# Five accumulator banks and three gate banks in the last stage of an attention, soft-MoE and SwiGLU kernel, with four smaller moves

## The chip, the cores and the metric

The kernel runs on one core of one Trainium2 chip. Times are device microseconds (us) of one execution. The core has a matrix engine (TensorE, PE in the listings, with its weight loads as PEld), VectorE (DVE), ScalarE (ACT), GpSimd (POOL) and a queue that issues the DMAs (SP). Each engine runs its own instructions in order and waits for the others by semaphores. Matmul results go to PSUM, which has eight banks of 512 fp32 numbers on each of 128 partitions.

## The reference

Three stages, all on 4608 tokens of width 512:

```python
# 1. attention in chunks of 64 rows, 64 heads-in-batch, D = 64
attn = softmax(scale * q_c @ k_c.T);  x = attn @ v_c
# 2. soft mixture of experts, 32 slots
logits = x @ phi
slot_input = softmax(logits, axis=0).T @ x
slot_out[e] = relu(slot_input[e] @ w1[e]) @ w2[e]
x = softmax(logits, axis=1) @ slot_out
# 3. gated feed-forward, 1536 hidden columns
g = x @ w_gate;  val = x @ w_val
out = (g * sigmoid(g) * val) @ w_out
```

The inputs `q`, `k`, `v`, `phi`, `w1` and `w2` come as fp32; the last three weights come as 64-bit floats and are turned into fp32 on the chip.

## The kernel before, in words

The instruction order on each engine is the order in which the program emits them (`tc.manual_schedule()`); tile pools place the semaphore waits. A pool with `bufs=n` hands out its n buffers in turn, and the first write to a buffer waits for the last reader of the tile that had it before.

**Stage 1 and 2 (up to about 171 us).** Attention is done in pairs of 128-token tiles; the slot logits of the nine 512-token groups are made along the way. After the last pair comes a tail in which little is left to overlap: the transposes `xt_ps` (L439) of the last tiles, the logits `lt_ps` (L458) of the last group, its maxima on DVE, the transposes `e_ps` (L504) and `mps` (L544). `warm(n)` (L571) multiplies the identity matrix with itself n times into a tile that nobody reads. Then come the experts (`h_ps`, `so_ps`).

**Hand-over (171 to 183 us).** `so_t` holds the slots' outputs. Since the third stage's input is `c @ slot_out`, the kernel multiplies the slots' outputs with `w_gate` and `w_val` first: `emit_g0` makes `gg_ps` (L853) for the first 256 hidden columns in two halves, and `evac_g` splits each into a high part (ACT copy, L846) and a remainder (DVE, L847) in `g_st`. The lambdas in `ev` do these evacuations. At the same time the first weights of `w_out` are converted: `exponents` (L200) and `mantissas` (L203) on DVE, `powers` (L218) on ACT, `sums` (L221) on DVE, then L232 and the product L253 or L246 on DVE or POOL, and for `w_out` the split L272 and L277.

**Stage 3 (from 174 us).** Work is cut into units (b, f): b is a block of 512 tokens, f one of twelve slices of 128 hidden columns; `SCHED` lists the order, so that a block does two or four slices in a row and comes back later. For each unit:

- `emit_gv`: `g_ps` and `v_ps` (L893), one matmul of 512 columns each, from the pool `ps_g`. ACT makes silu of the first (L896), DVE multiplies by the second (L897) into `s_sb`.
- `emit_hi`, `emit_lo`: `s_sb` is split into `hi_sb` (ACT, L903) and `lo_sb` (POOL, L910).
- `emit_out`: twelve products (L937) in four rows of three, `hi*w_hi`, `hi*w_lo`, `lo*w_hi`. Row t adds into accumulator tile t, from the pool `ps_o`. On the last slice of a block's visit each row is added into `part` by DVE (L952), or on the first visit copied there by DVE and ACT in turn (L954, L956).

The loop emits in step n the gate products of unit n, the split of unit n-1, one step of the weight conversion, and the products of unit n-2. The rest of `w_gate` and `w_val` comes in five chunks c = 1 to 5. When a chunk has been converted into `gw` (POOL, L246), `emit_ga` makes `ga_ps`, four narrow matmuls (L864) side by side on 32 columns each, whose result ACT and DVE split (L868, L870), and a step later `emit_gb` adds the four parts up with two matmuls (`gb_ps`, L877) and `evac_g` empties it. `try_g` decides which of the two is due; it is called from inside `emit_out`, through `subs`, a list of (row, function). `ga_ps` and `gb_ps` come from `ps_g` too.

Of the kernel before, what the change touches and what calls it, by code (L numbers as in the profile page):

```python
# [34 lines left out]
def tile_attn_softmoe_swiglu(  # L35
# [270 lines left out]
    with tc.manual_schedule():  # L306
# [145 lines left out]
        def emit_lmm(g, lt=None):  # L452
            if lt is None:
                lt = ps_t.tile([128, 512], F32, tag="t", name="lt_ps")
            lt_t[g] = lt
            for kk in range(4):
                for jt in range(4):
                    nc.tensor.matmul(  # L458
                        out=lt[32 * jt:32 * jt + 32, 0:128],
                        lhsT=phi_sb[:, kk, :],  # L460
                        rhs=xt_t[4 * g + jt][:, kk, :],
                        start=(kk == 0), stop=(kk == 3),
                        tile_position=(0, 32 * jt),
                    )

        def emit_lmax(g):
            lt = lt_t[g]
            mx = sm.tile([128, 1], F32, tag="mx", name="mx")
            mn = sm.tile([128, 1], F32, tag="mn", name="mn")
            nc.vector.tensor_reduce(out=mx, in_=lt[:, 0:128], axis=AX.X, op=ALU.max)  # L470
            if g:
                nc.vector.tensor_scalar(out=mn, in0=mx, scalar1=mrun[0], scalar2=-1.0, op0=ALU.max, op1=ALU.mult)
            else:
                nc.vector.tensor_scalar(out=mn, in0=mx, scalar1=-1.0, scalar2=None, op0=ALU.mult)
            if g:
                nc.vector.tensor_tensor(out=mx, in0=mx, in1=mrun[0], op=ALU.max)
            lx_t[g] = mn, mrun[0]
            mrun[0] = mx

        def emit_lexp(g):  # L480
            lt = lt_t[g]
            mn, old = lx_t.pop(g)
            et = atp.tile([128, 128], F32, tag="et", name="et", bufs=1)
            z = sm.tile([128, 1], F32, tag="z", name="z")
            nc.scalar.activation(out=et, in_=lt[:, 0:128], func=ACTF.Exp, bias=mn, accum_out=z)
            if g:
                be = sm.tile([128, 1], F32, tag="be", name="be")
                nc.scalar.activation(out=be, in_=old, func=ACTF.Exp, bias=mn)
                beta_t[g] = be
            if g < NG - 1:  # L490
                nc.scalar.activation(out=lt_all[:, g, :], in_=lt[:, 0:128], func=ACTF.Copy)
            et_t[g] = et, z
# [8 lines left out]
        def emit_et(g, sums=True):  # L501
            et, z = et_t[g]
            ps = ps_t.tile([128, 512], F32, tag="t", name="e_ps")
            nc.tensor.transpose(ps[:, 0:128], et, ident)  # L504
            e = atp.tile([128, 128], F32, tag="e", name="e", bufs=1)
            nc.scalar.activation(out=e, in_=ps[:, 0:128], func=ACTF.Copy)
            e_t[g] = e
            if sums:
                emit_zst(g)
# [110 lines left out]
        emit_lmax(g - 1)  # L620
        emit_xt(NTILE - 1)
        emit_lexp(g - 1)
        emit_lmm(g, lt2[:, 1])
        emit_et(g - 1, False)
        emit_lmax(g)
        emit_lexp(g)
        emit_zst(g - 1)
# [204 lines left out]
        nc.vector.tensor_copy(out=so_t[:, 2:4, 0:96], in_=sot_ps[1][:, :, 0:96])  # L832
        pp.close()
        pq.close()
        ps_o = ctx.enter_context(tc.tile_pool(name="ps_o", bufs=4, space=PSUM, reuse_waits="tile"))
        ps_g = ctx.enter_context(tc.tile_pool(name="ps_g", bufs=4, space=PSUM, reuse_waits="tile"))
        ht2 = ctx.enter_context(tc.tile_pool(name="ht2", bufs=3, side="right"))
        g_st = ht2.tile([128, NSC, 2, 256], F32R, name="g_st", bufs=1)
        sel_r = ht2.tile([128, 128], F32R, name="sel_r", bufs=1)
# [34 lines left out]
        def emit_gb(c):  # L874
            gp = ps_g.tile([128, 2, 256], F32, tag="g", name="gb_ps")
            for i, x in enumerate(gs_t.pop(c)):
                nc.tensor.matmul(out=gp.rearrange("p a f -> p (a f)"), lhsT=sel_r, rhs=x, start=(i == 0), stop=(i == 1))  # L877
            evac_g(gp, g_st[:, c])
# [7 lines left out]
        def emit_gv(b, f, parts=1):  # L886
            c, ff = f // 2, (f % 2) * 128
            gp = ps_g.tile([128, 512], F32, tag="g", name="g_ps")
            vp = ps_g.tile([128, 512], F32, tag="g", name="v_ps")
            s = ht2.tile([128, 512], F32, tag="s", name="s_sb", bufs=2)  # L890
            for ps, gi in ((gp, 0), (vp, 1)):
                for k in cols(parts):
                    nc.tensor.matmul(out=ps[:, k], lhsT=g_st[:, c, gi, ff:ff + 128], rhs=c_blk(b)[:, k],  # L893
                                     start=True, stop=True)
            for k in cols(parts):
                nc.scalar.activation(out=s[:, k], in_=gp[:, k], func=ACTF.Silu)  # L896
                nc.vector.tensor_tensor(out=s[:, k], in0=s[:, k], in1=vp[:, k], op=ALU.mult)  # L897
            s_t[b, f] = s
# [81 lines left out]
        ev[0]()  # L980
        ev[1]()
        exponents()
        emit_gv(*gvs[0], 2)
        mantissas()
        ev = [emit_g0(1, i, ps_g, "g") for i in range(2)]
        conv_d(nc.gpsimd)
        emit_hi(*gvs[0], 2)
        powers, sums = conv_b_parts()
        ev[0]()
        sums()  # L990
        ev[1]()
        powers()
        emit_lo(*gvs[0], nc.vector, 2)
        conv_c(nc.vector)
# [7 lines left out]
        emit_lo(*gvs[1], nc.vector, 2)  # L1002
        g_done = [1]

        def try_g(pos):
            c = g_done[0]
            if c in gs_t:
                emit_gb(c)
                g_done[0] += 1
            elif c < NSC and pos >= 6 * c + 4:  # L1010
                emit_ga(c)

        LAG = 2
# [8 lines left out]
        for n in range(1, len(seq) + LAG):  # L1022
            if n < len(seq):
                c = gvs[n][1] // 2
                conv_until(6 * c + 4)
                while g_done[0] <= c:
                    try_g(conv_pos())
            pos = conv_pos()
            if 1 < n < len(seq) and n != 3:
                emit_gv(*gvs[n])  # L1030
            if 3 < n <= len(seq):
                emit_hl(*gvs[n - 1], nc.gpsimd)
            m = 1 if n == 2 else n - LAG if n > 3 else None
            start = 36 - len(conv_q) < RATE * n + R0
            subs = [(1, lambda: try_g(pos))]
            if n < len(seq):
                if m is not None and seq[m][3]:
                    conv_step(start, "dc")
                    if seq[m][0] in part:
                        subs.append((3, lambda: conv_step(start, "ba")))  # L1040
                    else:
                        subs += [(1, lambda: conv_step(start, "b")), (3, lambda: conv_step(start, "a"))]
                else:
                    conv_step(start)
            if n == 2:
                subs += [(0, lambda: emit_hl(*gvs[2], nc.gpsimd)), (1, lambda: emit_gv(*gvs[3]))]
            if m is not None:
                out_step(m, subs)
            if n == 4:
                emit_sel()  # L1050
# [51 lines left out]
```

## Time and profile before

| what | value |
|---|---|
| median of three timed runs | 540.0 us (539.29 to 544.04) |
| the profiled execution | 540.84 us, of which the span of the records is 539.1 us |
| PE busy | 520.0 us, 96% of the span |
| DVE, ACT, POOL busy | 75%, 47%, 44% of the span |
| mean granted TensorE clock | 0.999 of full speed |

The span runs from the first to the last recorded instruction; 1.7 us of the profiled execution lie around it. Busy shares are means over the whole span: DVE is busy for nine tenths of the time between 185 and 410 us and for under half of it afterwards.

### The profile page before, as it was taken

Reading aid. Unit: us, or ns where it says so; the run is one execution under the profiler, and the core shown is the slowest. Engines: PE = TensorE matmul, PEld = TensorE weight load, DVE = VectorE, ACT = ScalarE, POOL = GpSimd, SP = SyncE. Lnnn points to the kernel's source line nnn. Section 1 sums busy time; section 2 is a strip of 40 time slices with the busy share of each in tenths; the row PEclk is TensorE's granted clock in tenths of the full one; section 3 lists DMA queues with packets and bytes.
Section 4 is the critical chain, followed back from the end, with each engine's and each line's share of the span. In section 5 each row is a group of like instructions: output and inputs, shape, how many; then the busy total and the mean of one; then the engine's idle time right before and its main releaser. Section 6 shows DMA issues by size and latency. Waiting matters only on the chain.

```text
span 539.1 us, 10978 instructions
## 1 busy us (share of the span) xinstructions
PE 520.0 (96%) x4359; PEld 401.9 (75%) x4359; DVE 402.5 (75%) x676; ACT 251.2 (47%) x491; POOL 235.8 (44%) x240
## 2 busy tenths in 40 slices
PE   7899999998999999999999999999999999999997
PEld 6777788874334788788787777777887888888885
DVE  5778888754766998898998988998988734444454
ACT  1344444333446766765454465455555433333331
POOL 3344443331002265655564556555555633443342
PEclk9999999999999999999999999999999999999999
DMA  8999999999999700222010222201000000222244
GB/s 319 403 354 398 341 397 356 402 415 392 406 416 413 327 1 0 80 78 80 0 54 25 79 78 78 80 4 75 0 1 0 2 1 2 78 79 95 98 181 172
DMA packets 23906, 91.09 MB, mean 169 GB/s; under 512 B 3120, under 2 KB 3120, under 8 KB 17968
## 3 DMA queue, kind: packets, MB, share of 16 engines
q1 hardware_dynamic: 23856, 90.40, 43.4%
q8 instruction: 34, 0.56, 0.4%
q14 instruction: 16, 0.13, 0.1%
HBM read 80.95 MB, written 9.44 MB: 168 GB/s over the span
## 4 chain that ended last, share of the span: by engine, by line
PE 88%; DVE 6%; ACT 2%; issue 2%; POOL 1%; DMA 1%; SPq 0%; ACTq 0%; POOLq 0%; DVEq 0%
PE o L937 52%; PE g_ps L893 4%; PE xa_ps L403 4%; PE v_ps L893 4%; PE xt_ps L439 3%; PE s_ps L366 3%; PE pt_ps L389 3%; PE so_ps L733 3%; PE h_ps L690 3%; PE si_ps L522 2%; PE xb_ps L403 1%; PE lt_ps L458 1%; PE ga_ps L864 1%; PE ct_ps L771 1%; DVE m L374 1%
## 5 line engine op out<-in xcount | busy, mean ns | idle before, releaser
L937 PE MATMUL o<-whl,hi_sb 128*128 128x512 f32 x864 | 267.3, 391 | 2.0 <-ACT s_sb L896 0.9
L910 POOL TENSOR_TENSOR lo_sb<-s_sb,hi_sb 128x512 fp32r<-128x512 f32 x106 | 140.0, 1322 | 147.2 <-ACT hi_sb L903 142.7
L937 PEld LDWEIGHTS o<-whl,hi_sb 128*128 128x128 f32 x864 | 161.1, 188 | 41.9 <-issue 6.3
L937 PE MATMUL o<-whl,lo_sb 128*128 128x512 f32 x432 | 168.1, 390 | 0.3 <-POOL lo_sb L910 0.3
L896 ACT ACTIVATE s_sb<-g_ps 128x512 f32<-128x512 f32 (+1 forms) x110 | 64.7, 590 | 151.6 <-PE g_ps L893 144.3
L897 DVE TENSOR_TENSOR s_sb<-s_sb,v_ps 128x512 f32<-128x512 f32 (+1 forms) x110 | 73.9, 674 | 75.9 <-ACT s_sb L896 74.7
L937 PEld LDWEIGHTS o<-whl,lo_sb 128*128 128x128 f32 x432 | 81.1, 188 | 18.2 <-POOL lo_sb L910 1.4
L903 ACT ACTIVATE hi_sb<-s_sb 128x512 fp32r<-128x512 f32 (+1 forms) x110 | 67.6, 616 | 0.2 <-DVE s_sb L897 0.2
L952 DVE TENSOR_TENSOR part<-part,o 128x512 f32<-128x512 f32 x100 | 62.2, 678 | 2.6 <-PE o L937 2.6
L356 POOL COPY vbd<-vbd 64x520 f32<-64x520 f32 x36 | 23.4, 651 | 70.1 <-DMA vbd<-in_v_dram 64.0
L232 DVE SCALAR_TENSOR_TENSOR ex<-raw,ex 128x512 uint16<-128x512 uint16 x32 | 50.1, 1566 | 0.0
L893 PE MATMUL v_ps<-c_t,g_st 128*128 128x512 f32 (+1 forms) x110 | 42.2, 387 | 0.7 <-DVE g_st L847 0.5
L893 PE MATMUL g_ps<-c_t,g_st 128*128 128x512 f32 (+1 forms) x110 | 42.3, 387 | 0.1
L391 ACT ACTIVATE pt<-pt_ps 128x512 f32<-128x512 f32 x36 | 19.5, 596 | 37.3 <-PE pt_ps L389 37.3
L221 DVE SCALAR_TENSOR_TENSOR mt<-mt,raw 128x512 f32<-128x512 f32 x32 | 36.3, 1133 | 0.1
L374 DVE TENSOR_REDUCE m<-s_ps 128x16 f32<-128x1024 f32 x18 | 22.0, 1225 | 16.3 <-PE s_ps L366 16.3
L246 POOL TENSOR_TENSOR gw<-mt,ex 128x512 f32<-128x512 f32 x20 | 24.6, 1229 | 16.1 <-PE g_ps L893 8.8
L203 DVE TENSOR_SCALAR mt<-raw 128x512 int32<-128x512 int32 x32 | 29.3, 914 | 0.0
L403 PE MATMUL xa_ps<-vbd,pt 128*64 128x130 f32 x432 | 28.2, 277 | 0.7 <-issue 0.7
L403 PEld LDWEIGHTS xa_ps<-vbd,pt 128*64 128x64 f32 x432 | 23.7, 135 | 3.4 <-issue 2.6
L441 ACT ACTIVATE xt<-xt_ps 128x512 f32<-128x512 f32 (+1 forms) x36 | 19.3, 596 | 14.5 <-PE xt_ps L439 11.0
L218 ACT ACTIVATE ex<-ex,cbias 128x512 uint16<-128x512 uint16 x32 | 22.9, 715 | 5.5 <-DVE ex L200 5.5
(141 smaller groups left out, 582.9 us busy)
## 6 DMA issues: line engine op xcount, KB each, us to landing
qk<-in_qk_dram SPq DMA_DIRECT2D x36, 512.0 KB, 6.5
w1t<-in_moe_w_dram SPq DMA_DIRECT2D x16, 1024.0 KB, 9.4
w2t<-in_moe_w_dram SPq DMA_DIRECT2D x15, 1024.0 KB, 13.5
vbd<-in_v_dram SPq DMA_DIRECT2D x36, 260.0 KB, 7.3
out_dram<-part SPq DMA_DIRECT2D x36, 256.0 KB, 2.2
raw<-in_moe_w_gate_dram SPq DMA_DIRECT2D x5, 1024.0 KB, 5.2
raw<-in_moe_w_val_dram SPq DMA_DIRECT2D x5, 1024.0 KB, 4.9
raw<-in_moe_w_out_dram SPq DMA_DIRECT2D x5, 1024.0 KB, 4.8
```

The costliest lines, as they stand in the source:

```text
L203: nc.vector.tensor_scalar(out=mt, in0=hw, scalar1=0xFFFFF, scalar2=0x41000000, op0=ALU.bitwise_and, op1=ALU.bitwise_or)
L221: nc.vector.scalar_tensor_tensor(out=m, in0=m, scalar=-7.0, in1=lw.bitcast(F32), op0=ALU.add, op1=ALU.add)
L232: nc.vector.scalar_tensor_tensor(out=ex, in0=hh, scalar=0x8000, in1=ex, op0=ALU.bitwise_and, op1=ALU.bitwise_or)
L374: nc.vector.tensor_reduce(out=m, in_=sv, axis=AX.X, op=ALU.max)
L403: nc.tensor.matmul(out=banks[n // 3][64 * cc:64 * cc + 64, (n % 3) * 2 * VW:(n % 3 + 1) * 2 * VW], lhsT=pt_t[i][:, j, 64 * cc:64 * cc + 64 ...
L893: nc.tensor.matmul(out=ps[:, k], lhsT=g_st[:, c, gi, ff:ff + 128], rhs=c_blk(b)[:, k], start=True, stop=True)
L896: nc.scalar.activation(out=s[:, k], in_=gp[:, k], func=ACTF.Silu)
L897: nc.vector.tensor_tensor(out=s[:, k], in0=s[:, k], in1=vp[:, k], op=ALU.mult)
L903: nc.scalar.activation(out=hi[:, k], in_=s_t[b, f][:, k], func=ACTF.Copy)
L910: eng.tensor_tensor(out=lo[:, k], in0=s[:, k], in1=hi[:, k].bitcast(F32), op=ALU.subtract)
L937: nc.tensor.matmul(out=acc_t[t], lhsT=x[:, t * 128:(t + 1) * 128], rhs=w, start=(first and i == 0), stop=(last and i == order[2]))
L952: nc.vector.tensor_tensor(out=p[:, t], in0=p[:, t], in1=acc_t[t], op=ALU.add)
```

## The change

Four edits, three of them in stage 3:

- `ps_o` has five banks in place of four, and `ps_g` three in place of four. The two `gg_ps` tiles of the second half are taken from `ps_o`.
- In the hand-over `mantissas()` is emitted ahead of the first unit's gate products, and both evacuations `ev[0]`, `ev[1]` ahead of `sums()`.
- `try_g` is called twice in a unit: behind the second row for `gb_ps` alone, behind the third row for `ga_ps` alone.
- Three and two identity products are added in the tail of stage 2.

```diff
@@ -620,8 +620,10 @@
         emit_xt(NTILE - 1)
         emit_lexp(g - 1)
+        warm(3, ps_x, "xb")
         emit_lmm(g, lt2[:, 1])
         emit_et(g - 1, False)
+        warm(2, ps_x, "xb")
         emit_lmax(g)
@@ -832,8 +834,8 @@
-        ps_o = ctx.enter_context(tc.tile_pool(name="ps_o", bufs=4, space=PSUM, reuse_waits="tile"))
-        ps_g = ctx.enter_context(tc.tile_pool(name="ps_g", bufs=4, space=PSUM, reuse_waits="tile"))
+        ps_o = ctx.enter_context(tc.tile_pool(name="ps_o", bufs=5, space=PSUM, reuse_waits="tile"))
+        ps_g = ctx.enter_context(tc.tile_pool(name="ps_g", bufs=3, space=PSUM, reuse_waits="tile"))
@@ -980,15 +982,15 @@
         exponents()
+        mantissas()
         emit_gv(*gvs[0], 2)
-        mantissas()
-        ev = [emit_g0(1, i, ps_g, "g") for i in range(2)]
+        ev = [emit_g0(1, i, ps_o, "o") for i in range(2)]
         conv_d(nc.gpsimd)
         emit_hi(*gvs[0], 2)
         powers, sums = conv_b_parts()
         ev[0]()
+        ev[1]()
         sums()
-        ev[1]()
         powers()
@@ -1002,12 +1004,13 @@
-        def try_g(pos):
+        def try_g(pos, which="ab"):
             c = g_done[0]
             if c in gs_t:
-                emit_gb(c)
-                g_done[0] += 1
-            elif c < NSC and pos >= 6 * c + 4:
+                if "b" in which:
+                    emit_gb(c)
+                    g_done[0] += 1
+            elif "a" in which and c < NSC and pos >= 6 * c + 4:
                 emit_ga(c)
@@ -1032,7 +1035,7 @@
-            subs = [(1, lambda: try_g(pos))]
+            subs = [(1, lambda: try_g(pos, "b")), (2, lambda: try_g(pos, "a"))]
```

The lines of the changed kernel below stand one to three higher than those of before. DVE in the hand-over, from the evacuation of the first half's `gg_ps` to the second unit's product, before:

```order
L847 TENSOR_TENSOR g_st<-gg_ps,g_st 32x128 x2
L200 TENSOR_SCALAR ex<-raw 128x512
L897 TENSOR_TENSOR s_sb<-s_sb,v_ps 128x256 x2
L203 TENSOR_SCALAR mt<-raw 128x512
L847 TENSOR_TENSOR g_st<-gg_ps,g_st 32x128
L221 SCALAR_TENSOR_TENSOR mt<-mt,raw 128x512
L847 TENSOR_TENSOR g_st<-gg_ps,g_st 32x128
L910 TENSOR_TENSOR lo_sb<-s_sb,hi_sb 128x256 x2
L232 SCALAR_TENSOR_TENSOR ex<-raw,ex 128x512
L253 TENSOR_TENSOR mt<-mt,ex 128x512
L897 TENSOR_TENSOR s_sb<-s_sb,v_ps 128x256 x2
```

and now:

```order
L849 TENSOR_TENSOR g_st<-gg_ps,g_st 32x128 x2
L200 TENSOR_SCALAR ex<-raw 128x512
L203 TENSOR_SCALAR mt<-raw 128x512
L899 TENSOR_TENSOR s_sb<-s_sb,v_ps 128x256 x2
L849 TENSOR_TENSOR g_st<-gg_ps,g_st 32x128 x2
L221 SCALAR_TENSOR_TENSOR mt<-mt,raw 128x512
L912 TENSOR_TENSOR lo_sb<-s_sb,hi_sb 128x256 x2
L232 SCALAR_TENSOR_TENSOR ex<-raw,ex 128x512
L253 TENSOR_TENSOR mt<-mt,ex 128x512
L899 TENSOR_TENSOR s_sb<-s_sb,v_ps 128x256 x2
```

L203 has moved ahead of the first unit's two products, and the two evacuations (L847, now L849) stand together ahead of the sum L221.

PE around the second of the five `ga_ps`, with its waits, from the second row's products of a block's last unit to the first product of the next block (`o_3707` and `o_3714` are the second row's tile; `DVE_49` and the like name the engine waited for), before:

```order
L937 MATMUL o_3707<-whl,hi_sb 128x512 x2
L937 MATMUL o_3707<-whl,lo_sb 128x512
L864 MATMUL ga_ps<-gw,so_t 32x512 x2
L864 MATMUL ga_ps<-gw,so_t 32x512 [waits Pool_49]
L864 MATMUL ga_ps<-gw,so_t 32x512
L937 MATMUL o_3711<-whl,hi_sb 128x512 x2
L937 MATMUL o_3711<-whl,lo_sb 128x512
L937 MATMUL o_3715<-whl,hi_sb 128x512 x2
L937 MATMUL o_3715<-whl,lo_sb 128x512
L893 MATMUL g_ps<-c_t,g_st 128x512 [waits DVE_49]
L893 MATMUL v_ps<-c_t,g_st 128x512 [waits Activation_49]
L937 MATMUL o_3772<-whl,hi_sb 128x512 [waits DVE_49,Activation_49]
```

and now:

```order
L939 MATMUL o_3714<-whl,lo_sb 128x512
L939 MATMUL o_3718<-whl,hi_sb 128x512 x2
L939 MATMUL o_3718<-whl,lo_sb 128x512
L866 MATMUL ga_ps<-gw,so_t 32x512 [waits DVE_49]
L866 MATMUL ga_ps<-gw,so_t 32x512
L866 MATMUL ga_ps<-gw,so_t 32x512 [waits Pool_49]
L866 MATMUL ga_ps<-gw,so_t 32x512
L939 MATMUL o_3722<-whl,hi_sb 128x512 x2
L939 MATMUL o_3722<-whl,lo_sb 128x512
L895 MATMUL g_ps<-c_t,g_st 128x512 [waits Activation_49]
L895 MATMUL v_ps<-c_t,g_st 128x512 [waits DVE_49]
L939 MATMUL o_3779<-whl,hi_sb 128x512 [waits Activation_49]
```

`ga_ps` stands one row later and waits for DVE as well as POOL; the first product of the next block has lost its wait for DVE, and `v_ps` behind a `ga_ps` waits for DVE.

PE in the tail of stage 2, a piece of the difference:

```order
 L439 MATMUL xt_ps<-ident,x_sb 128x128 x8
+L574 MATMUL warm<-ident 128x128 x3
 L458 MATMUL lt_ps<-xt,phi_sb 32x128 x16
 L504 MATMUL e_ps<-ident,et 128x128
+L574 MATMUL warm<-ident 128x128 x2
 L544 MATMUL mps<-ident,mx 1x128
```

The identity products stand between the transposes of the last tiles and the logits made from them, and ahead of the transpose of the maxima.

## Rows read from the trace of the kernel before

**Rows 1.** The page: busy time of PE; granted clock in 40 slices.

```profile
PE 520.0 (96%) x4359; PEld 401.9 (75%) x4359; DVE 402.5 (75%) x676; ACT 251.2 (47%) x491; POOL 235.8 (44%) x240
...
PEclk9999999999999999999999999999999999999999
```

**Rows 2.** Chain that ended last: start, length, engine, tile; two units undisturbed.

```profile
428.72 2.72 PE o L937 x12
431.90 2.72 PE o L937 x12
```

**Rows 3.** Timeline, 284 to 287 us: start, length, line, count, [idle before <-releaser].

```profile
284.28 1.80 DVE L232 SCALAR_TENSOR_TENSOR ex<-raw,ex 128x512 uint16<-128x512 uint16 x1
...
286.00 1.27 DVE L952 TENSOR_TENSOR part<-part,o 128x512 f32<-128x512 f32 x2
...
285.99 0.39 PE L893 MATMUL v_ps<-c_t,g_st 128*128 128x512 f32 x1
286.83 0.70 PE L937 MATMUL o<-whl,hi_sb 128*128 128x512 f32 x2 [0.45 <-DVE part L952]
```

**Rows 4.** Timeline of PE at 306 us.

```profile
305.95 0.61 PE L937 MATMUL o<-whl,hi_sb 128*128 128x512 f32 x2
306.72 0.50 PE L937 MATMUL o<-whl,lo_sb 128*128 128x512 f32 x1 [0.15 <-POOL lo_sb L910]
```

**Rows 5.** Timeline of the hand-over, all engines.

```profile
171.91 0.42 DVE L203 TENSOR_SCALAR mt<-raw 128x512 int32<-128x512 int32 x1
...
175.95 0.75 DVE L897 TENSOR_TENSOR s_sb<-s_sb,v_ps 128x256 f32<-128x256 f32 x2
...
176.52 1.27 POOL L277 TENSOR_TENSOR whl<-mt,whl 128x512 fp32r<-128x512 f32 x1 [0.93 <-ACT whl L272]
176.62 1.46 DVE L203 TENSOR_SCALAR mt<-raw 128x512 int32<-128x512 int32 x1
...
177.66 0.28 ACT L846 ACTIVATE g_st<-gg_ps 128x128 fp32r<-128x128 f32 x1 [0.35 <-PE gg_ps L853]
...
179.16 0.29 DVE L847 TENSOR_TENSOR g_st<-gg_ps,g_st 32x128 fp32r<-32x128 f32 x1
...
181.59 0.75 DVE L897 TENSOR_TENSOR s_sb<-s_sb,v_ps 128x256 f32<-128x256 f32 x2
...
182.59 1.20 PE L937 MATMUL o<-whl,hi_sb 128*128 128x512 f32 x4 [0.30 <-ACT hi_sb L903]
```

**Rows 6.** Timeline at the second and the third `ga_ps`.

```profile
262.41 1.28 POOL L246 TENSOR_TENSOR gw<-mt,ex 128x512 f32<-128x512 f32 x1 [1.83 <-ACT hi_sb L903]
...
262.69 2.10 PE L864 MATMUL ga_ps<-gw,so_t 128*32 128x512 f32 x8
...
311.03 1.07 PE L864 MATMUL ga_ps<-gw,so_t 128*32 128x512 f32 x8
```

**Rows 7.** Timeline of PE and POOL, 367 to 376 us.

```profile
367.86 0.39 PE L893 MATMUL v_ps<-c_t,g_st 128*128 128x512 f32 x1
...
370.21 0.73 PE L937 MATMUL o<-whl,hi_sb 128*128 128x512 f32 x2 [0.32 <-DVE part L952]
...
375.78 0.39 PE L937 MATMUL o<-whl,lo_sb 128*128 128x512 f32 x1
...
374.02 1.29 POOL L910 TENSOR_TENSOR lo_sb<-s_sb,hi_sb 128x512 fp32r<-128x512 f32 x1 [2.12 <-ACT hi_sb L903]
```

**Rows 8.** Timeline of the tail of stage 2.

```profile
125.47 1.08 PE L458 MATMUL lt_ps<-xt,phi_sb 128*32 128x128 f32 x32 [1.02 <-ACT lt_all L491]
...
127.56 0.27 PE L544 MATMUL mps<-ident,mx 128*1 128x128 f32 x1 [0.76 <-DVE zst L514]
...
130.45 0.94 PE L574 MATMUL warm<-ident 128*128 128x128 f32 x6
```

**Rows 9.** Timeline at 261 us, PE and DVE.

```profile
261.01 0.39 PE L893 MATMUL v_ps<-c_t,g_st 128*128 128x512 f32 x1
...
261.05 0.67 DVE L897 TENSOR_TENSOR s_sb<-s_sb,v_ps 128x512 f32<-128x512 f32 x1
```

## The prediction

> **What bounds the kernel now.** I read the page first. TensorE (PE) is busy for 96% of the span, and the clock row shows 9 in every slice [rows 1], so only PE's pauses can be won, and part of its 19 idle us lies where the edit does not reach. In the last stage a unit (twelve `o` products, and the `g_ps` and `v_ps` of a later unit: 14 products at 0.23 us) takes 3.17 us when nothing stops it [rows 2]; no edit shortens that. Then I went through PE's timeline behind 171 us for starts that stand further apart than 0.23 us. The bracketed waits alone are not enough: at 286.83 the bracket says 0.45, but the product starts 0.84 behind `v_ps` [rows 3], because the bracket counts from the end of the product before. The pauses are of four kinds: the hand-over into the last stage (177 to 183 us), one `ga_ps` that waits for POOL, four block changes that wait for an accumulator bank, and two products that wait for `lo_sb`, at 306.72 [rows 4] and again at 347.7, which the change does not touch. The first three kinds sum to about 5.5 us, the most that can come back.
>
> **Hand-over (mantissas earlier, both evacuations ahead of the sum).** L203 takes 0.42 us while POOL rests, but 1.46 at 176.62, where it starts 0.10 behind POOL's L277 and ends when that has ended [rows 5]. Behind it in DVE's queue stand both L847, for which PE waits; the second ends at 179.45. In the new order L203 has the place of the two L897, at 175.95, and ends at 176.37, before POOL starts at 176.52. That takes 1.04 us out of DVE's queue, but not all of it counts. The L897 move to 176.35 and `hi_sb` with them, still in time for PE, which has `gg_ps` to do until 177.4. The second L847 cannot start before its ScalarE copy L846 ends at 177.94 [rows 5], so it ends at 178.26, and L221, L910, L232 and L253 follow (0.32, 0.70, 0.68 and 0.72 from start to start, as before). The second unit's L897 comes to 181.11 in place of 181.59, and the product at 182.59, which waits for the `hi_sb` made from it [rows 5], to 182.10. What is late next is still DVE, with its sum, power and product ahead of that L897. Gain **0.48**; bounds 0, if ScalarE is later than I put it, and 1.04, the whole of L203.
> The Trainium skill (SBUF — State Buffer, "Who interferes with whom") says that VectorE in a two-port mode and GpSimd exclude each other for a whole instruction, and the second to issue waits. By that rule too the new place costs 0.42, and the sum stays.
> The two `gg_ps` tiles of this place now come from the five-bank pool, so the fourth `o` tile waits for the first L847, which ends at about 177.95; that product's own turn is at 178.1. No cost.
>
> **`ga_ps` behind the third row.** Four of the five take 1.07 us like the one at 311.03. The one at 262.69 takes 2.10, since its second half waits for the `gw` that POOL writes from 262.41 to 263.69 [rows 6]. Three products more ahead of it (3 x 0.23 = 0.68) use up part of that wait, and its end stays where it was: **0.68** gained, once. Bounds 0 and 1.03. `gb_ps` now comes 11 products (2.5 us) behind `ga_ps` in place of 14, and in between lie two evacuations like L952's 0.67 [rows 3], so it waits for nothing.
>
> **Five accumulator banks.** With four, the first product of a block needs the bank of the old block's first row, whose sum L952 stands on DVE behind a long L232: 284.28 to 286.08, L952 from 286.00, the product at 286.83 in place of 286.22. The pair that starts there also takes 0.70 [rows 3] in place of 0.61 [rows 4], so 0.70 is lost. The same pattern stands at 327.76 and 407.70. With the fifth bank the first row needs none of these sums. The second, 0.68 later at 286.90, needs the sum that now releases the first at 286.83. The two sums shown take 1.27, so they follow each other in 0.60, faster than PE's rows, and later rows are free too: 3 x 0.70 = **2.1**.
> At 368 us it is different. By its turn the third row would start at 369.45 (`v_ps` at 367.86 and seven products); it starts at 370.21 [rows 7], and with the slow restart 0.86 is lost. The fifth bank removes that, but the fourth row, whose turn is at 370.13, then needs the sum for which the third waits now (370.21): 0.2 with the restart. And the `lo_sb` that POOL writes from 374.02 to 375.31, which hangs on a DVE queue that is full all the way from 365.7, is read at 375.78 [rows 7]: 0.47 of slack against 0.67 won, and a restart. Of 0.86 there stay **0.3**. Bounds for the four together: 0 (all given back later) and 3.0.
>
> **Three gate banks.** `v_ps` now takes the bank of the `g_ps` before, which ScalarE empties half a unit later; `g_ps` takes that of the `v_ps` two units back. Around `ga_ps` and `gb_ps` it is one unit, but one lengthened by those products. I take **0**; the price of the other end comes with the slower rival.
>
> **Identity products.** Three stand in PE's pause ahead of 125.47 (1.02 us) and two in the one ahead of 127.56 (0.76) [rows 8]. Three such products take 0.94, so two take 0.63: both fit, at **0**. With no pause to cover them they would cost 1.6. For a gain the clock would have to fall near there, and its row has 9 throughout [rows 1], so none.
> The Trainium skill (TensorE: Matmul & The Clock Gate, Part 1) says that idleness puts the array at half clock and that activity releases it, which speaks for such fillers; here the trace shows no fall that they could prevent, and by the rule too the sum is 0.
>
> **Sum.** 0.48 + 0.68 + 2.1 + 0.3 = 3.6 us. Profiled execution: 540.84 - 3.6 = 537.2. That execution lies 0.84 above the median of the three timed runs; from the median of 540.0 the forecast is **536.4**, 0.7% less.
>
> **Rivals.**
> *DVE gives the bank time back.* DVE is the late engine at each of these places. If its queue stays late by as much, the pause moves from the first row to a later `lo_sb`, as I expect at 375.78. Then only the hand-over and `ga_ps` count: 540.0 - 1.2 = 538.8. Against it: at 286.83 PE waits for one sum only, and DVE's sums run faster than PE's rows [rows 3]. Chance 0.15.
> *DVE and POOL meet in another order.* PE's earlier starts may change which of the two comes first. The long L203 [rows 5], the long L232 [rows 3] and the late `lo_sb` at 306.72 [rows 4] rest on that order: that `lo_sb` product starts 0.77 behind the pair before it, in place of 0.45, and with the restart 0.4 is lost. If both such pauses and the 0.56 given back at 368 us go: 540.0 - 3.6 - 1.4 = 535.0. Chance 0.08.
> The rule of the skill's SBUF page above would make each such switch all or nothing for one instruction.
> *Three gate banks bind (slower).* Mechanism: `v_ps` waits for the L897 of the unit before. One such L897 runs from 261.05 to 261.72, with the next `v_ps` at 261.01 [rows 9]: 0.7 late, 0.8 with a restart. It decides if the pool's turn makes `v_ps` follow the last `v_ps` in ordinary units: five units as late as this eat the gain, seven give 540.0 - 3.6 + 5.6 = 542.0. Against it: in the order of the changed kernel `v_ps` waits for DVE only next to `ga_ps` and `gb_ps`, elsewhere for ScalarE. Chance 0.05.
> *Nothing moves*: 540.0, if the pauses of this one profiled execution are not those of the timed ones. Chance 0.04.
>
> **How the numbers follow.** The forecast (535.2 to 537.9) has 0.68. The range takes in the first rival and reaches to the second: 534.9 to 540.0 leaves out the slower rival and the tails. About 1% (5.4 us) is what a measurement of this kernel can tell from no change; the most that the change can win is 5.5. So *faster* by that much has 0.05, *slower* 0.04, *same* 0.91.
>
> **What would show it.** In the profile after: L203 at 0.42, ahead of POOL's L277, and the product of 182.59 half a microsecond earlier; all five `ga_ps` at 1.1 to 1.5; the first product of each block 0.23 behind its `v_ps`; a smaller pause left near 370 or 375; the two `lo_sb` pauses as before; 124 to 131 us as long as before; no wait of `v_ps` or `g_ps`. Waits at the gate products, or pauses that move on to `lo_sb`, would make it wrong.

## The result, and the profile after

| what | before | changed |
|---|---|---|
| median of 13 runs each, us | 541.57 (539.29 to 544.13) | 537.35 (536.14 to 539.11) |
| ratio | | 0.9918, 95% interval 0.9897 to 0.9939 |
| the profiled execution / its span, us | 540.84 / 539.1 | 536.63 / 534.9 |
| last stage: first output product to the last record, us | 361.68 | 358.45 |

The forecast was 536.4, in a range of 534.9 to 540.0, and 3.6 us less than before. Measured are 4.2 less; the interval goes from 3.3 to 5.6. In absolute terms the changed kernel came 0.95 above the forecast, because that starts from the median of three runs (540.0) and the thirteen runs of the kernel before have 541.57. The two profiled executions also differ by 4.2 us in span, but only part of that is the change's. I compared the start of each unit's first output product in the one trace with the start of the same product in the other (units are counted from 0; a shift is noted where it first shows):

| stretch | what lies in it | shift, us |
|---|---|---|
| up to the last transposes at 123 us | attention, not touched | -0.91 |
| 123 to 176 us | identity products, experts | -0.06 |
| to the second unit's first product | hand-over | -0.58 |
| units 26 and 27 | second `ga_ps`, then a wait of `v_ps` | -0.68, then +0.42 |
| units 32, 44 and 68 | first product of a block | -0.66, -0.72, -0.77 |
| units 56 to 59 | the block change at 368 us | -0.68, then +0.43 |
| last stage in all | | -3.23 |

The 0.91 ahead of the edits is chance: in the fourteen profiled executions of this study the last transpose starts anywhere from 122.8 to 125.6 us, and both ends belong to kernels whose attention is the same. So what the trace can vouch for is 3.3 us, at the near end of the measured interval. The medians hold one thing more that these two traces cannot show; it comes with the identity products below.

The page after: PE is busy for as long as before, in a shorter span, at the same clock [rows 1].

```profile
PE 520.0 (97%) x4369; PEld 403.8 (75%) x4369; DVE 401.7 (75%) x676; ACT 251.9 (47%) x491; POOL 235.4 (44%) x240
...
PEclk9999999999999999999999999999999999999999
```

The hand-over after, as a timeline (start, length, engine, line; compare [rows 5]):

```profile
174.82 0.41 DVE L203 TENSOR_SCALAR mt<-raw 128x512 int32<-128x512 int32 x1
...
175.26 0.75 DVE L899 TENSOR_TENSOR s_sb<-s_sb,v_ps 128x256 f32<-128x256 f32 x2
175.54 1.28 POOL L277 TENSOR_TENSOR whl<-mt,whl 128x512 fp32r<-128x512 f32 x1 [0.93 <-ACT whl L272]
...
176.66 0.62 DVE L849 TENSOR_TENSOR g_st<-gg_ps,g_st 32x128 fp32r<-32x128 f32 x2 [0.65 <-ACT g_st L848]
...
180.05 0.75 DVE L899 TENSOR_TENSOR s_sb<-s_sb,v_ps 128x256 f32<-128x256 f32 x2
...
181.04 1.19 PE L939 MATMUL o<-whl,hi_sb 128*128 128x512 f32 x4 [0.69 <-ACT hi_sb L905]
```

L203 is over before GpSimd's L277 begins and takes 0.41 in place of 1.46. The second unit's product, which stood 5.21 behind the first output product, now stands 4.63 behind it (176.41 to 181.04). It still waits for `hi_sb`: DVE's queue is what is late next.

The first of the block changes, after (compare [rows 3]):

```profile
282.46 1.79 DVE L232 SCALAR_TENSOR_TENSOR ex<-raw,ex 128x512 uint16<-128x512 uint16 x1
...
284.19 2.47 DVE L954 TENSOR_TENSOR part<-part,o 128x512 f32<-128x512 f32 x4
284.19 0.39 PE L895 MATMUL v_ps<-c_t,g_st 128*128 128x512 f32 x1
...
284.42 0.62 PE L939 MATMUL o<-whl,hi_sb 128*128 128x512 f32 x2
```

DVE is as late as before: the long L232 ends at 284.25, the sums follow it. But the product starts 0.23 behind `v_ps`, since with a fifth bank it needs none of them. The same stands at 324.67 and 403.62.

The second `ga_ps` and what follows it (compare [rows 6]):

```profile
261.80 1.43 PE L866 MATMUL ga_ps<-gw,so_t 128*32 128x512 f32 x8
...
265.92 1.57 DVE L221 SCALAR_TENSOR_TENSOR mt<-mt,raw 128x512 f32<-128x512 f32 x1
...
267.41 0.68 DVE L899 TENSOR_TENSOR s_sb<-s_sb,v_ps 128x512 f32<-128x512 f32 x1
...
268.14 0.50 PE L895 MATMUL v_ps<-c_t,g_st 128*128 128x512 f32 x1 [0.15 <-DVE s_sb L899]
```

`ga_ps` takes 1.43 in place of 2.10. But the next unit's `v_ps`, whose turn is at 267.83 (0.23 behind its `g_ps`), starts at 268.14: its bank is that of the `v_ps` before, and L899, which reads that one, is held up behind the long L221. The product behind it follows in 0.34 in place of 0.23 as well, so that 0.42 is lost. This is the wait that I had put at nothing.

Near 370 us (compare [rows 7]):

```profile
366.28 1.29 DVE L954 TENSOR_TENSOR part<-part,o 128x512 f32<-128x512 f32 x2
...
367.02 0.74 PE L939 MATMUL o<-whl,hi_sb 128*128 128x512 f32 x2
...
367.43 1.30 POOL L277 TENSOR_TENSOR whl<-mt,whl 128x512 fp32r<-128x512 f32 x1
367.48 1.53 DVE L200 TENSOR_SCALAR ex<-raw 128x512 uint16<-128x512 uint16 x1
...
370.86 1.29 POOL L912 TENSOR_TENSOR lo_sb<-s_sb,hi_sb 128x512 fp32r<-128x512 f32 x1 [2.12 <-ACT hi_sb L905]
...
372.20 0.50 PE L939 MATMUL o<-whl,lo_sb 128*128 128x512 f32 x1
```

The fourth row (367.02) starts 0.07 late, which with the product behind it costs 0.18, and the `lo_sb` product of a later unit (372.20) starts 0.05 behind the end of L912 and about 0.3 behind its turn, as forecast. The two pauses at `lo_sb` that the change does not touch are there as before [rows 4], the first of them here:

```profile
301.50 1.28 POOL L246 TENSOR_TENSOR gw<-mt,ex 128x512 f32<-128x512 f32 x1 [1.83 <-ACT hi_sb L905]
...
302.74 1.47 POOL L912 TENSOR_TENSOR lo_sb<-s_sb,hi_sb 128x512 fp32r<-128x512 f32 x1
...
304.26 0.50 PE L939 MATMUL o<-whl,lo_sb 128*128 128x512 f32 x1 [0.16 <-POOL lo_sb L912]
```

### The profile page after: what moved, and what is told of

The parts are those of the page before. It is cut to its first block, busy times and chain, and to the rows that moved or that the text cites. A ratio compares the mean times of both kernels' runs of the same rounds, so it can differ in the third digit from the quotient of the medians.

```text
span 534.9 us, 10971 instructions
## 1 busy us (share of the span) xinstructions
PE 520.0 (97%) x4369; PEld 403.8 (75%) x4369; DVE 401.7 (75%) x676; ACT 251.9 (47%) x491; POOL 235.4 (44%) x240
## 4 chain that ended last, share of the span: by engine, by line
PE 86%; DVE 8%; ACT 2%; issue 2%; POOL 1%; ACTq 0%; POOLq 0%; DVEq 0%
PE o L939 50%; PE xa_ps L403 4%; PE v_ps L895 4%; PE g_ps L895 4%; PE s_ps L366 3%; PE xt_ps L439 3%; PE pt_ps L389 3%; PE so_ps L735 3%; PE h_ps L692 3%; PE si_ps L522 2%; DVE part L954 2%; PE xb_ps L403 1%; PE lt_ps L458 1%; PE ct_ps L773 1%; DVE m L374 1%
## 5 line engine op out<-in xcount | busy, mean ns | idle before, releaser
L912 POOL TENSOR_TENSOR lo_sb<-s_sb,hi_sb 128x512 fp32r<-128x512 f32 x106 | 140.5, 1326 | 142.3 <-ACT hi_sb L905 138.3
L899 DVE TENSOR_TENSOR s_sb<-s_sb,v_ps 128x512 f32<-128x512 f32 (+1 forms) x110 | 74.0, 674 | 72.4 <-ACT s_sb L898 71.2
L954 DVE TENSOR_TENSOR part<-part,o 128x512 f32<-128x512 f32 x100 | 62.3, 679 | 2.6 <-PE o L939 2.6
L232 DVE SCALAR_TENSOR_TENSOR ex<-raw,ex 128x512 uint16<-128x512 uint16 x32 | 49.6, 1548 | 0.0
L221 DVE SCALAR_TENSOR_TENSOR mt<-mt,raw 128x512 f32<-128x512 f32 x32 | 36.9, 1155 | 0.1
L246 POOL TENSOR_TENSOR gw<-mt,ex 128x512 f32<-128x512 f32 x20 | 24.6, 1231 | 16.1 <-PE g_ps L895 8.1
L203 DVE TENSOR_SCALAR mt<-raw 128x512 int32<-128x512 int32 x32 | 28.3, 884 | 0.0
```

Source lines behind the costliest of these rows:

```text
L203: nc.vector.tensor_scalar(out=mt, in0=hw, scalar1=0xFFFFF, scalar2=0x41000000, op0=ALU.bitwise_and, op1=ALU.bitwise_or)
L221: nc.vector.scalar_tensor_tensor(out=m, in0=m, scalar=-7.0, in1=lw.bitcast(F32), op0=ALU.add, op1=ALU.add)
L232: nc.vector.scalar_tensor_tensor(out=ex, in0=hh, scalar=0x8000, in1=ex, op0=ALU.bitwise_and, op1=ALU.bitwise_or)
L912: eng.tensor_tensor(out=lo[:, k], in0=s[:, k], in1=hi[:, k].bitcast(F32), op=ALU.subtract)
L954: nc.vector.tensor_tensor(out=p[:, t], in0=p[:, t], in1=acc_t[t], op=ALU.add)
```

## The experiments

Each kernel has a ratio to before, and a last stage from its own trace, taken as above (two subtractions of times in one trace, so that the chance in attention falls out). In units that an edit does not reach the traces agree within about 0.1 us, far closer than the times do.

| kernel | last stage, us | ratio to before, 95% interval |
|---|---|---|
| before | 361.68 | 1 |
| changed | 358.45 | 0.9918 (0.9897 to 0.9939) |
| hand-over alone | 361.11 | 0.998 (0.9954 to 1.0007) |
| narrow products alone | 361.04 | 0.9982 (0.9962 to 1.0003) |
| five and three banks alone | 359.31 | 0.9952 (0.9927 to 0.9977) |
| changed, no identity products | 358.46 | 0.994 (0.9907 to 0.9973) |
| changed, four and four banks | 360.47 | 0.9961 (0.9941 to 0.998) |
| changed, two identity products for five (one execution) | 358.42 | |
| changed, nine identity products for three | 358.38 | 0.9943 (0.9924 to 0.9963) |
| changed, six and two banks | 365.87 | 1.0069 (1.0048 to 1.0091) |
| changed, all 20 L246 on VectorE | 358.12 | 0.9924 (0.9899 to 0.9948) |
| changed, nothing on GpSimd | 359.19 | 0.9955 (0.9937 to 0.9973) |
| changed, 14 of the L246 on VectorE | 356.69 | 0.9909 (0.9886 to 0.9932) |
| the same, L277 on VectorE too | 357.58 | 0.9903 (0.9867 to 0.9938) |

**The edits one by one.** To the kernel before, the hand-over alone:

```diff
         exponents()
+        mantissas()
         emit_gv(*gvs[0], 2)
-        mantissas()
...
         ev[0]()
+        ev[1]()
         sums()
-        ev[1]()
```

> The kernel before with the hand-over edit alone (mantissas ahead of the first gate products, both evacuations ahead of the sum; four and four banks). The theory that the edits act each by itself: counted from the first output product, the second unit's first product comes 0.58 us earlier than before (5.21 before, 4.63), and nothing else in the last stage moves, so the three block changes still stop PE for 0.7 each and the time is 0.6 us below before. The rival that the hand-over's gain is used up by the queues behind it: the 0.58 is gone again by the first narrow gate products, 35 us later.

Measured: 0.58 at the second unit's first product, 0.57 at the end; the block changes stop PE as before. The rival falls.

The narrow products alone, with four gate banks:

```diff
-            subs = [(1, lambda: try_g(pos))]
+            subs = [(1, lambda: try_g(pos, "b")), (2, lambda: try_g(pos, "a"))]
```

> The kernel before with the narrow gate products behind the third row alone, and four gate banks. If it was the third gate bank that gave back 0.42 us in the changed kernel (v_ps waiting for VectorE's product right behind the second ga_ps), the second ga_ps gains 0.68 here and all of it lasts to the end: last stage 0.68 shorter than before. The rival, that VectorE is late there whatever the banks: PE stops behind that ga_ps here too, at a product of the next unit, and 0.26 lasts.

Measured: 0.70 at unit 26, and 0.64 at the end. PE's rows at the second `ga_ps`:

```profile
264.70 1.43 PE L864 MATMUL ga_ps<-gw,so_t 128*32 128x512 f32 x8
...
270.51 0.39 PE L893 MATMUL g_ps<-c_t,g_st 128*128 128x512 f32 x1
...
270.74 0.39 PE L893 MATMUL v_ps<-c_t,g_st 128*128 128x512 f32 x1
```

`v_ps` follows `g_ps` in 0.23: with four gate banks it waits for nothing.

The banks alone, with the second half's `gg_ps` from `ps_o`:

```diff
-        ps_o = ctx.enter_context(tc.tile_pool(name="ps_o", bufs=4, space=PSUM, reuse_waits="tile"))
-        ps_g = ctx.enter_context(tc.tile_pool(name="ps_g", bufs=4, space=PSUM, reuse_waits="tile"))
+        ps_o = ctx.enter_context(tc.tile_pool(name="ps_o", bufs=5, space=PSUM, reuse_waits="tile"))
+        ps_g = ctx.enter_context(tc.tile_pool(name="ps_g", bufs=3, space=PSUM, reuse_waits="tile"))
-        ev = [emit_g0(1, i, ps_g, "g") for i in range(2)]
+        ev = [emit_g0(1, i, ps_o, "o") for i in range(2)]
```

> The kernel before with five accumulator and three gate banks alone. If the block changes are stopped by the bank and nothing else, the first product of a block follows its v_ps by 0.23 at the three places, 0.66 to 0.77 us each, and the place near 368 gives 0.25: the last stage 2.4 us shorter than before, less what a gate product loses at a ga_ps (at most 0.5). The rival, that VectorE gives the time back: pauses of PE at lo_sb or at later rows, under 1.2 us in all.

Measured: 2.37, with 0.60, 0.72 and 0.77 at the three block changes and 0.23 near 368; nothing is lost at a `ga_ps`, and nothing in the hand-over. The three parts sum to 0.57 + 0.64 + 2.37 = 3.58, the whole gives 3.23. Three gate banks alone cost nothing and the later `ga_ps` alone costs nothing; together they cost the 0.42.

**The identity products.** The changed kernel without them:

```diff
-        warm(3, ps_x, "xb")
...
-        warm(2, ps_x, "xb")
```

> The changed kernel without the five identity products. If they are covered, the time from the last transposes to the first expert product is the same within 0.1 us and the total within 0.5 us of the changed kernel. The rival, that the products (or the order of code that they bring) shortened the stages ahead of the last one, where the changed kernel's trace was 0.9 us ahead by 118 us: the last group's logits come 0.9 us later again, and the time is 1 us above the changed kernel.

Measured: from the start of the last group's final logits product to the first expert product 6.33 in place of 6.23, the same last stage, and a last transpose at 123.25 as in the changed kernel. In the traces the products bring 0.10, and the 0.9 ahead of them is not theirs. The time does not fit what was expected: the median of seven is 538.54, 1.2 above the changed kernel in place of at most 0.5, as the rival had it, though the intervals of the two ratios overlap.

A likelier source of the rival's number stands on record with each execution: the mean granted TensorE clock. Five of the seven have 0.997 or more and a median of 536.96; the other two have 0.992 and take 539.16 and 541.93 us. All the executions of this study whose clock is on record, sorted by it:

| kernels | executions | of them at 0.992 to 0.994 |
|---|---|---|
| without identity products at these places (before, each edit alone, changed without them) | 120 | 25 |
| with them (changed and all its other variants, one execution with the pair alone) | 70 | 0 |

All others have 0.996 or more. Of one kernel on one chip, the executions at 0.992 to 0.994 take 2 to 4 us longer in the median than the others. On the three chips that are known to have run both kinds it is 8 of 47 against 0 of 57. So by these counts the identity products do more than the 0.10: no kernel with them has such an execution. Why is not shown. No kept trace is of one of the 25, and in all fourteen the clock is full until the last 2.1 us, so that neither the stretch in which it falls nor the group of products that prevents it can be named.

The other way, nine for three:

```diff
-        warm(3, ps_x, "xb")
+        warm(9, ps_x, "xb")
```

> The changed kernel with nine identity products in place of three ahead of the last group's logits. Nine take 9 x 0.22 = 2.0 us behind the last transpose, and the pause covers 1.2 of them: from the last transpose to the end of the logits 0.8 us more than in the changed kernel (2.10 to 2.9), and all of it reaches the end of the stage. The rival, that such fillers cost nothing while TensorE has to wait in the tail anyway (later pauses swallow them): under 0.3 us at the first expert product.

Measured: from the last transpose to the last logits product 3.02 in place of 2.10, and no later pause takes any of the 0.92 back. Three fit and nine don't: the pause is the whole cover. Then the pair alone:

```diff
-        warm(3, ps_x, "xb")
```

> The changed kernel without the three identity products ahead of the last logits, the two ahead of the transpose of the maxima kept. In five traces with both groups, the time from the last group's logits to the first expert product is 6.23 to 6.24 us, in five without any 6.32 to 6.33. If the group of two brings that 0.10 (the transpose of the maxima starts 0.06 behind the maxima in place of 0.15), it is 6.23 here; the rival, that it is the group of three: 6.33.

Measured in a single execution (536.15 us): 6.33. So the 0.10 needs the group of three, though it shows behind the group of two: the transpose of the maxima starts 0.15 behind the maxima without the three, 0.06 with the three. Whether the three alone bring it was not run, and why they do, I cannot say.

**What the banks decide.** The changed kernel with four and four again:

```diff
-        ps_o = ctx.enter_context(tc.tile_pool(name="ps_o", bufs=5, space=PSUM, reuse_waits="tile"))
-        ps_g = ctx.enter_context(tc.tile_pool(name="ps_g", bufs=3, space=PSUM, reuse_waits="tile"))
+        ps_o = ctx.enter_context(tc.tile_pool(name="ps_o", bufs=4, space=PSUM, reuse_waits="tile"))
+        ps_g = ctx.enter_context(tc.tile_pool(name="ps_g", bufs=4, space=PSUM, reuse_waits="tile"))
```

> The changed kernel with four accumulator and four gate banks again (all else of the change kept). If the accumulator bank brings the block changes and the third gate bank costs one wait of 0.42 us at the second ga_ps, the last stage (first output product to the end) takes 361.68 - 0.57 - 0.64 = 360.5 us, 2.0 longer than in the changed kernel: block changes stop PE again, v_ps behind the second ga_ps waits for nothing. The rival, that this wait comes from VectorE being late whatever the banks: v_ps or the product behind it still loses 0.4 there, last stage 360.9.

Measured: 360.47. `v_ps` waits for nothing at the second `ga_ps`, the four block changes stop PE, and the rival falls. And the other way, six and two:

```diff
-        ps_o = ctx.enter_context(tc.tile_pool(name="ps_o", bufs=5, space=PSUM, reuse_waits="tile"))
-        ps_g = ctx.enter_context(tc.tile_pool(name="ps_g", bufs=3, space=PSUM, reuse_waits="tile"))
+        ps_o = ctx.enter_context(tc.tile_pool(name="ps_o", bufs=6, space=PSUM, reuse_waits="tile"))
+        ps_g = ctx.enter_context(tc.tile_pool(name="ps_g", bufs=2, space=PSUM, reuse_waits="tile"))
```

> The changed kernel with six accumulator and two gate banks. If the rule for a gate bank is that v_ps waits for the product L899 that last read its bank, then with two banks every v_ps waits for the L899 of the unit before, which in the changed kernel's trace ends behind the next v_ps's start in seven units (0.39 to 1.89, 5.3 us in all), and next to the five ga_ps and gb_ps for VectorE's L872 and L849 (0.4 to 1.6 each, some 7 us in all); part is relieved, since PE's pauses let VectorE catch up: last stage 6 to 13 us longer than in the changed kernel. The rival, that a sixth accumulator bank pays for it (block changes near 368 us, where 0.43 is left) and VectorE catches up: under 2 us longer.

Measured: 365.87, 7.4 us longer, near the low end of what I expected. The group of `v_ps` in the view by lines, its idle time before it and what ended that:

```profile
L895 PE MATMUL v_ps<-c_t,g_st 128*128 128x512 f32 (+1 forms) x110 | 44.0, 403 | 6.6 <-DVE s_sb L899 3.5 <-DVE glo L872 2.2 <-DVE g_st L849 0.9
```

In the changed kernel this group has 0.3. So the slower rival of the prediction names a real mechanism; it decides with two gate banks, and with three only at one place.

**What makes VectorE late.** The pauses that are left behind the hand-over (the wait of `v_ps`, the two at `lo_sb` and the 0.43 at 372) I put down to long VectorE instructions next to GpSimd's, or to GpSimd's own queue. First, the 20 products of `gw` on VectorE:

```diff
-            nc.gpsimd.tensor_tensor(
+            nc.vector.tensor_tensor(
                 out=gw_t[c][:, 2 * u:2 * u + 2, "gv".index(kind)], in0=m.rearrange("p (k f) -> p k f", k=2),
```

> The changed kernel with the 20 products that make gw (L246) on VectorE in place of GpSimd. If VectorE's L203 is long (1.4 in place of 0.42) because it starts against GpSimd's L246, all the L203 that follow an L246 go to 0.42, which pays for 0.69 more per product; GpSimd's remainder is free 1.3 us earlier, so the two lo_sb pauses of 0.4 at 304 and 344 and the 0.36 that the second ga_ps still waits go: last stage 357.3, 1.1 shorter than in the changed kernel. The rival, that VectorE is too full: L203 stays long or sums come later, and new pauses of over 1 us at L899, v_ps or the block changes.

Half right. Both `lo_sb` pauses, the rest of the second `ga_ps`'s wait and that of `v_ps` are gone, which gives 0.79 at the second `ga_ps` and behind it and 0.46 at each `lo_sb`. But two block changes stop PE again for 0.7 each, so that 0.33 is left. One of them:

```profile
285.77 0.69 DVE L246 TENSOR_TENSOR gw<-mt,ex 128x512 f32<-128x512 f32 x1
...
286.38 2.47 DVE L954 TENSOR_TENSOR part<-part,o 128x512 f32<-128x512 f32 x4
...
287.12 0.72 PE L939 MATMUL o<-whl,hi_sb 128*128 128x512 f32 x2 [0.40 <-DVE part L954]
```

Where L246 stands ahead of a block's sums it delays them by its own 0.6, and the second row finds no free bank. Then all that GpSimd does behind the hand-over on VectorE (products L246 and L253, splits L277, remainders L912):

```diff
-            nc.gpsimd.tensor_tensor(
+            nc.vector.tensor_tensor(
...
-        (eng or nc.gpsimd).tensor_tensor(out=m, in0=m, in1=p, op=ALU.mult)
+        (eng or nc.vector).tensor_tensor(out=m, in0=m, in1=p, op=ALU.mult)
...
-        eng = eng or (nc.vector if n_d[0] % 2 else nc.gpsimd)
+        eng = eng or nc.vector
...
-                emit_hl(*gvs[n - 1], nc.gpsimd)
+                emit_hl(*gvs[n - 1], nc.vector)
```

> The changed kernel with everything that GpSimd does behind 183 us (remainders lo_sb, products, splits) on VectorE. If VectorE's long instructions (L232 at 1.8, L221 at 1.2, L203 at 1.4) are long because they start against GpSimd, every L232 takes 0.68, L221 0.69 and L203 0.42; VectorE saves about 58 us by 410 us and takes on about 72, so it is nearly full (217 of 225 us) and the last stage is 0 to 5 us longer than in the changed kernel. The rival, that they are long by themselves: they stay, VectorE needs 275 us for 225, and the last stage is over 30 us longer.

Measured: 0.74 longer than the changed kernel, since VectorE, now nearly full, stops PE at new places, for 0.6 to 0.9 each: at a bank (274.15 us) and twice at its own `lo_sb` (277.81 and 371.71). VectorE's groups by line from 183 to 425 us (count, then busy us and mean ns of one), in the changed kernel

```profile
L232 DVE SCALAR_TENSOR_TENSOR ex<-raw,ex 128x512 uint16<-128x512 uint16 x30 | 48.2, 1606 | 0.0
L221 DVE SCALAR_TENSOR_TENSOR mt<-mt,raw 128x512 f32<-128x512 f32 x30 | 35.6, 1185 | 0.0
L954 DVE TENSOR_TENSOR part<-part,o 128x512 f32<-128x512 f32 x56 | 34.8, 677 | 0.0
L203 DVE TENSOR_SCALAR mt<-raw 128x512 int32<-128x512 int32 x30 | 27.5, 915 | 0.0
```

and with GpSimd at rest:

```profile
L912 DVE TENSOR_TENSOR lo_sb<-s_sb,hi_sb 128x512 fp32r<-128x512 f32 (+1 forms) x74 | 50.1, 678 | 1.2 <-ACT hi_sb L905 1.2
...
L954 DVE TENSOR_TENSOR part<-part,o 128x512 f32<-128x512 f32 x56 | 34.9, 681 | 0.0
L221 DVE SCALAR_TENSOR_TENSOR mt<-mt,raw 128x512 f32<-128x512 f32 x30 | 20.6, 686 | 0.0
L232 DVE SCALAR_TENSOR_TENSOR ex<-raw,ex 128x512 uint16<-128x512 uint16 x30 | 20.6, 685 | 0.0
...
L203 DVE TENSOR_SCALAR mt<-raw 128x512 int32<-128x512 int32 x30 | 12.6, 421 | 0.0
```

The three groups fall from 111.3 to 53.8 us. The sums L954, which read PSUM, take 0.68 in both. The rival, that the instructions are long by themselves, is out. The Trainium skill (SBUF — State Buffer, "Who interferes with whom") says that a VectorE instruction with two inputs in SBUF contends with a GpSimd one that reads SBUF, that one in a two-port mode contends with GpSimd too, and that outside these modes one with at most one such input does not. The rows agree for L232 and L221, which have two inputs in SBUF, and for L954, which has one. L203 has one too and is long beside GpSimd all the same, so by that page it would have to run in a two-port mode, which the trace does not show.

From these two runs a version follows: L246 on VectorE only in the 14 steps where L200 and L203 are queued behind it.

```diff
-            nc.gpsimd.tensor_tensor(
+            (eng or nc.gpsimd).tensor_tensor(
...
             if k in which and stage[k]:
-                f()
+                f(nc.vector) if k == "c" and "a" in which and stage[k][0][0] != "o" else f()
```

> The changed kernel with L246 on VectorE in the 14 steps where L200 and L203 are queued behind it, and on GpSimd where only the sums of a block's end are (6). With all 20 on VectorE the last stage gained 1.06 at the second ga_ps and the wait behind it, 0.9 at the two lo_sb, and lost 0.7 at each of two block changes, where L246 stood ahead of the sums. If that is all, the gains stay and the losses go: last stage 358.12 - 1.4 = 356.7, 1.7 below the changed kernel, total 535.7. The rival, that the queue at the block ends shifts with the places before them: a block change still loses over 0.5, last stage 357.5 or more.

(The 1.06 in this text is counted from the kernel before; from the changed kernel it is 0.79.)

Measured: 356.69, and a median of 536.11 against 540.38 of before on the same chip. GpSimd and VectorE at the second `ga_ps` in the changed kernel:

```profile
260.85 1.27 POOL L246 TENSOR_TENSOR gw<-mt,ex 128x512 f32<-128x512 f32 x1 [1.83 <-ACT hi_sb L905]
...
261.03 1.38 DVE L203 TENSOR_SCALAR mt<-raw 128x512 int32<-128x512 int32 x1
```

VectorE and PE at the same place now:

```profile
261.12 0.69 DVE L246 TENSOR_TENSOR gw<-mt,ex 128x512 f32<-128x512 f32 x1
...
262.06 0.42 DVE L203 TENSOR_SCALAR mt<-raw 128x512 int32<-128x512 int32 x1
...
262.98 1.06 PE L866 MATMUL ga_ps<-gw,so_t 128*32 128x512 f32 x8
```

The same product that took GpSimd 1.27, with an L203 beside it that ended only 0.29 after it, costs VectorE 0.69 and gives back 0.96 at L203. The last stage is 1.76 us shorter than that of the changed kernel; the intervals of the two ratios overlap, so the times alone do not part them. At last, L277 of the loop on VectorE as well:

```diff
-        eng = eng or (nc.vector if n_d[0] % 2 else nc.gpsimd)
+        eng = eng or nc.vector
```

> The kernel with the 14 products on VectorE (last stage 356.69), and all of the splits L277 of the loop on VectorE as well. Near 368 VectorE's L200 takes 1.53 next to GpSimd's L277, and this makes lo_sb late by 0.4 at 371. With L277 on VectorE (0.69 more there) L200 takes 0.42, lo_sb comes 0.5 earlier, the 0.43 that the place gives back goes: last stage 356.3, everything else as it was. The rival, that VectorE has no room at four other places where it takes on an L277: last stage 356.7 or longer.

Measured: the place near 370 gives back nothing any more (0.43 won), 0.2 is lost around 281, and from the first to the last output product it is 352.29 us, against 352.50. Yet the last stage is 357.58, which by the number on record is on the rival's side: it is 5.3 us from the start of the last product to the last record, where the other thirteen executions have 4.2 to 4.3. The work ends in the last stores, and whether their delay belongs to the kernel is open; its time (536.0) is that of the version before.

## Why the prediction was right, and the two steps that failed

- **Hand-over:** forecast 0.48, measured 0.58. L203 beside a resting GpSimd took what it was put at, and the second `L849` ended as worked out. DVE's queue behind it was 0.1 quicker: L912 started 0.61 behind L221, where 0.70 was put.
- **Second `ga_ps`:** forecast 0.68, and the unit behind it was 0.68 earlier.
- **Three gate banks:** forecast 0, measured 0.42 lost, once. The first step that failed is "I take 0": the text named the places next to `ga_ps` where `v_ps` waits for DVE, and had a row for a late L899, but did not put the two together with its own term. PE came 0.68 earlier to a `v_ps` whose bank is emptied by a queue that did not become earlier. Rows of L899 against the *shifted* turn of `v_ps` would have shown it.
- **Block changes:** forecast 0.70 each, measured 0.66, 0.72 and 0.77.
- **The place at 368:** forecast 0.3 net of 0.86; measured 0.25, that is 0.68 won (0.18 of the 0.86 goes at the fourth row) and 0.43 given back at `lo_sb`, the two rows that the text names.
- **Identity products:** forecast 0, measured 0.10 won in the traces, for a reason that stays open. The second step that failed is that no gain was to be had from them since the clock "has 9 throughout": that is the row of one execution. Of 120 executions without these products 25 have a lower mean clock and are 2 to 4 us longer, of 70 with them none.

So the three edits of the last stage, run alone, sum to 3.58 against a forecast of 3.56; that sum was wrong only in taking them to be independent, and errors of up to 0.1 on either side cancel in it. The medians differ by 4.2, which is 0.9 more than the traces show behind the start of the tail. Nothing in the forecast gives that 0.9. Executions at the lower clock are a candidate for part of it: from the counts above (a fifth of the executions, about 3 us each) they make some 0.6 us of the mean, an estimate. For the thirteen executions of before the clocks are not on record, but four of them lie above 543 us, and none of the changed kernel's above 539.2.

Of the rivals, "DVE gives the bank time back" came true at 372 alone, by about the amount that the forecast had, and "Three gate banks bind" at one place, for 0.42. The two `lo_sb` pauses stayed.

## What to carry to other kernels

When several edits bring one engine forward, work out each wait again at the shifted time, since a buffer's user may come earlier while its last reader does not. One trace is one execution: what happens in a fifth of them has to be looked for in the list of all. An accumulator bank more pays where its last reader stands behind a long instruction, and the bank is best taken from the pool whose readers are early; a second one taken from there cost 7.4 us here. Before an instruction is moved to the idle engine, look at whose instructions get longer while it runs: 14 of GpSimd's products were cheaper on the busier VectorE.

## What the runs showed of the hardware

- VectorE's L200 started 0.05 behind GpSimd's L277 (1.30) and took 1.53, ending 0.28 behind it; without GpSimd it takes 0.42. I read this as waiting until the other was over, shown as busy.
- After a wait, the product behind the first one follows in 0.30 to 0.34 us in place of 0.23, at every place behind 190 us in the traces of before and of the changed kernel; a wait of 0.3 costs 0.4.
- In 25 of 120 executions without the identity products of the tail the mean granted clock was 0.992 to 0.994 and the time 2 to 4 us longer; with them it was 0.997 or more in all 70.
- Attention moved by 2.8 us between executions (122.8 to 125.6), while the last stage repeated within 0.1 in kernels that share its code (358.38 to 358.46). Differences under half a per cent are seen in such a stage, not in the total.
